# Transposing K on VectorE instead of TensorE in a one-core decode kernel, and sending one row block of a weight to half of the partitions

## The chip, the cores and the metric

The kernel runs on one core of a Trainium2 chip. The metric is device time in microseconds (us) of one execution; lower is better. The kernel before the change takes 134.09 us (median of three runs, 134.08 to 134.11). The profiled execution spans 132.1 us; all positions in time below are microseconds from the start of that span. TensorE is called PE in the profile, VectorE is DVE, ScalarE is ACT, GpSimd is POOL, and SyncE, which issues most of the transfers, is SP.

## What is computed

One decode step of a transformer layer for a batch of two tokens: attention over a sliding window of a cache, and a two-layer perceptron, both fed by the same normalised token, and added to it.

```python
# x: [2, 1, 576]; 32 query heads, 16 key/value heads of 128; the last 2048 positions of an 8192-long cache
xn = layernorm(x)
q = (xn @ wq)                                   # wq: [576, 4096]
scores = q . k_cache[:, :, 6144:, :] * 128**-0.5   # each key/value head serves two query heads
p = softmax(scores); o = p . v_cache[:, :, 6144:, :]
attn = o.reshape(2, 1, 4096) @ wo               # wo: [4096, 576]
h = relu(xn @ w1 + b1) ** 2                     # w1: [576, 4608]
mlp = h @ w2 + b2                               # w2: [4608, 576]
out = x + attn + mlp
```

All inputs are bf16. The windows of K and V are 16.8 MB each and the four weights together 20 MB, so 53.6 MB are read for very little arithmetic. (In the kernel the term x is left to the product with `sel_b`, which adds x and b2 in one matmul.)

## The kernel before

The work on the cache is cut into eight *units*: unit u holds four key/value heads of one batch element, 2 MB of K and 2 MB of V. A tile of K has 128 partitions of 64 positions times 128 elements. K must be transposed so that the head dimension lies on the partitions; the kernel before does that on TensorE, two bf16 values at a time viewed as one fp32, into PSUM, and copies the result to SBUF alternately with ScalarE and VectorE:

```python
kvpool = ctx.enter_context(tc.tile_pool(name="kvpool", bufs=6))      # six tiles for K and V together

def transposes(u, g):                            # g = 0..7
    k_f = k_tiles[u][:].bitcast(F32)
    kT_ps = psum.tile([P, JG * P], BF16, tag="kT", bufs=3, ...)
    for i in range(JG // 2):                     # four 128x128 fp32 transposes
        transpose(out=kT_f[:, i * P:(i + 1) * P], in_=k_f[:, j * P:(j + 1) * P], identity=ident_f[:])
    ...
    (nc.scalar.copy if g % 2 == 0 else nc.vector.tensor_copy)(out=kT, in_=kT_ps[:])

def scores(u, t):                                # t = 0, 1: half a unit; 8 matmuls each, four side by side
    ...
    for c in range(2):
        for g in range(4):
            matmul(sc_ps[32 * g:32 * (g + 1), :], lhsT=qz[:, tq, b, c, z:z + SR],
                   rhs=kT[:, :, 32 * g:32 * (g + 1), c], ..., tile_position=(0, 32 * g))

def softmax(u):
    # VectorE: m1 = max of the scores, m2; GpSimd: gmax = max over partitions; VectorE: gown, bias
    # ScalarE: p = exp(scale * scores + bias);  VectorE: pT = transpose(p)  (32x32 blocks)

def step(u):
    for g in range(NG):
        transposes(u, g)
        # at g = 1, 2: pv(u - 2), the product with V, and pv_end(u - 2), four VectorE operations on it
        # at g = 5: scores(u, 0);  at g = 6: fin of unit u - 2 (a matmul op_ps, then linv, om, ws on VectorE)
    scores(u, 1)
    softmax(u)
```

After unit 6 the first layer of the perceptron runs (`mlp_h`: matmuls h_ps with w1, relu on ScalarE, the square `hrow` on VectorE, its transposes `hp`, copies to `hT_sb`). Only then can the tile of w1 be given to wo. The rest of the program:

```python
mlp_h(w1_sb)
wo_sb = issue_flat(A_wo, "wo")                   # takes the buffer of w1
...                                              # w2a: first half of w2; w2b, w2c (three pieces): second half
step(NU - 1)                                     # unit 7
pv_all(NU - 2); pv_all(NU - 1)                   # V of units 6 and 7
for r in range(WR):  out_acc(ws[:, r, :], wo_sb, r)           # 128 matmuls, need `ws` of unit 7
for r in range(FR):  out_acc(hT_sb[:, 0, r, :], w2a_sb, r)    # 72 matmuls
for r in range(FR):  out_acc(hT_sb[:, 1, r, :], ...)          # 36 with w2b, 36 with w2c
nc.scalar.copy(out=fin_sb[:], in_=out_ps[:])
nc.scalar.dma_start(out=out_v, in_=fin_sb[0:RM:BS, :])
```

Each half of w2 has 18 rows (of 576 bf16, 1,152 bytes) for each of the 128 partitions. `out_acc` is four matmuls of 144 columns. Transfers are issued on SyncE's queue in this order: k0, wq, k1, v0, k2, v1, k3, v2, k4, v3, k5, v4, k6, v5, w1, k7, v6, v7, wo, w2a, w2b, w2c in three pieces.

## Time and profile before

| what | value |
|---|---|
| time, median of three runs | 134.09 us |
| span of the profiled execution | 132.1 us |
| read from HBM | 53.62 MB, 406 GB/s over the span |
| busy: PE, DVE, ACT, POOL | 84.6, 63.2, 46.7, 4.9 us |
| mean granted clock of PE | 0.834 |

The table is a summary of the page of the profile. A busy PE is not a PE at its peak, because matmuls overlap and their ends are modelled. The page's second part cuts the span into 40 slices of 3.3 us and gives the busy share of each engine in tenths; the row DMA is the mean share of the 16 transfer engines, and the row GB/s what they moved. The chain of waits follows the work that ended last backwards, from each step to what released it. A view by stretches of time gives, for any stretch, each engine's busy time with the number of instructions in brackets, then PE's granted clock, the DMA share and GB/s; its shares can pass 1 a little, since a packet counts where it starts.

### The profile page before, as it was taken

The page shows a single profiled execution, that of the slowest core. Times are in us where ns is not written, and L with a number is a line of the kernel's source. Part 1 is how long each engine was busy: PE and PEld are TensorE (multiplying, and loading weights), DVE is VectorE, ACT ScalarE, POOL GpSimd, SP SyncE. Part 2 cuts the span into 40 slices and gives each one's busy share as a digit, 9 for nine tenths or more (in the row PEclk, how much of TensorE's full clock was granted, in tenths as well). Part 3 has the DMA queues.
Part 4 walks back from the last instruction along what each step waited for, and adds up shares of the span by engine and source line. Part 5 has one row for each costly group of instructions (what it writes and reads, how often), then busy time and mean ns, then how long its engine had stood idle before and what let it go on. Part 6 is the DMA issues. An engine that isn't in the chain of part 4 may idle for free.

```text
span 132.1 us, 2285 instructions
## 1 busy us (share of the span) xinstructions
PE 84.6 (64%) x949; PEld 52.6 (40%) x949; DVE 63.2 (48%) x176; ACT 46.7 (35%) x67; POOL 4.9 (4%) x15
## 2 busy tenths in 40 slices
PE   0089319599589687697599787104819972739471
PEld 0069202286345353363455443002417640229360
DVE  7764400344557677396547687410075667550000
ACT  5725400339566085283256094200106632000000
POOL 5000000010010100100100100100000001000000
PEclk9999955959999999999779999855695999555955
DMA  4999899999999999999999999999999999899960
GB/s 160 397 437 526 369 388 442 422 432 432 429 432 422 442 417 427 437 432 437 432 427 414 437 488 402 445 424 405 427 427 442 468 435 458 376 408 418 418 255 1
DMA packets 3511, 53.76 MB, mean 407 GB/s; under 512 B 419, under 2 KB 558, under 8 KB 814
## 3 DMA queue, kind: packets, MB, share of 16 engines
q1 hardware_dynamic: 3456, 53.61, 95.2%
q8 instruction: 7, 0.11, 0.3%
q10 hardware_dynamic: 46, 0.02, 0.1%
q14 instruction: 2, 0.02, 0.0%
HBM read 53.62 MB, written 0.00 MB: 406 GB/s over the span
## 4 chain that ended last, share of the span: by engine, by line
DMA 78%; PE 15%; ACT 2%; SPq 1%; DVE 1%; issue 1%; ACTq 0%; DVEq 0%
DMA w<-in_B_w_dram 25%; DMA w2c<-in_B_w_dram 24%; DMA k<-in_A_k_cache_dram 16%; DMA wq<-in_A_wq_dram 13%; PE kT_ps L97 5%; PE h_ps L94 3%; PE q_ps L94 3%; PE sc_ps L94 2%; PE out_ps L94 1%; PE o_ps L94 1%; ACT kT L270 1%; DVE qrow L238 1%; SPq L106 0%; ACT qrow L238 0%; DVE qz L254 0%
## 5 line engine op out<-in xcount | busy, mean ns | idle before, releaser
L97 PE MATMUL kT_ps<-ident_f,k 128*128 128x128 f32 x256 | 41.4, 312 | 5.7 <-DMA k<-in_A_k_cache_dram 3.9
L97 PEld LDWEIGHTS kT_ps<-ident_f,k 128*128 128x128 f32 x256 | 32.9, 161 | 18.8 <-issue 9.9
L270 ACT COPY kT<-kT_ps 128x1024 bf16<-128x1024 bf16 x32 | 31.9, 1012 | 17.8 <-PE kT_ps L97 17.8
L272 DVE COPY kT<-kT_ps 128x1024 bf16<-128x1024 bf16 x32 | 21.8, 682 | 6.4 <-PE kT_ps L97 6.1
L94 PE MATMUL sc_ps<-kT,qz 128*32 128x512 bf16 x128 | 9.9, 388 | 6.7 <-DVE kT L272 4.7
L302 ACT ACTIVATE p<-sc_ps,bias 128x512 bf16<-128x512 f32 x8 | 5.5, 688 | 21.4 <-DVE gown L298 18.2
L94 PE MATMUL o_ps<-v,pT 128*32 128x512 bf16 x128 | 11.2, 429 | 0.0
L94 PEld LDWEIGHTS <-xnT 128*4 128x4 bf16 x108 | 3.5, 121 | 16.8 <-issue 15.2
L94 PE MATMUL h_ps<-w,xnT 128*4 128x288 bf16 x72 | 4.3, 429 | 8.0 <-DMA w<-in_B_w_dram 8.0
L305 DVE STREAM_TRANSPOSE pT<-p 128x512 bf16<-128x512 bf16 x8 | 5.7, 710 | 6.2 <-ACT p L302 6.2
L335 DVE SCALAR_TENSOR_TENSOR o<-o_ps,in_s,o 128x128 f32<-128x128 f32 x24 | 8.3, 345 | 0.4
L291 DVE TENSOR_REDUCE m<-sc_ps 128x1 f32<-128x512 f32 x8 | 5.5, 692 | 4.8 <-PE sc_ps L94 4.8
L375 DVE TENSOR_TENSOR hrow<-t 100x1152 bf16<-100x1152 f32 x2 | 2.6, 1355 | 9.6 <-ACT t L373 9.6
L94 PE MATMUL q_ps<-wq,xnT 128*4 128x512 bf16 x36 | 4.0, 627 | 4.9 <-DMA wq<-in_A_wq_dram 4.9
L295 POOL PARTITION_ALL_REDUCE gmax<-m x8 | 2.9, 367 | 104.9 <-DVE m L293 104.9
L94 PE MATMUL op_ps<-o,of_h 128*32 128x129 f32 x16 | 3.7, 316 | 4.6 <-DVE o L335 4.6
L456 ACT CAST fin_sb<-out_ps 113x144 bf16<-113x144 f32 x1 | 0.3, 280 | 17.9 <-PE out_ps L94 17.9
L94 PEld LDWEIGHTS <-qz 128*32 128x32 bf16 x128 | 2.1, 94 | 10.4 <-DVE kT L272 7.2
L97 PE MATMUL pro_ps<-ident,xn_sb 2*128 2x2 bf16 x5 | 0.9, 182 | 6.8 <-DVE xn_sb L171 6.5
L94 PEld LDWEIGHTS <-hT_sb 128*17 128x17 bf16 x144 | 3.4, 108 | 3.6 <-issue 3.5
L94 PE MATMUL out_ps<-wo,ws 128*17 128x144 bf16 x128 | 4.0, 325 | 1.2 <-DVE ws L351 1.2
L238 DVE CAST qrow<-q_ps 100x512 bf16<-100x512 f32 x1 | 0.7, 692 | 8.2 <-PE q_ps L94 8.2
(71 smaller groups left out, 57.4 us busy)
## 6 DMA issues: line engine op xcount, KB each, us to landing
k<-in_A_k_cache_dram SPq DMA_DIRECT2D x8, 2048.0 KB, 21.0
v<-in_A_v_cache_dram SPq DMA_DIRECT2D x8, 2048.0 KB, 21.5
w<-in_B_w_dram SPq DMA_DIRECT2D x1, 5184.0 KB
wq<-in_A_wq_dram SPq DMA_DIRECT2D x1, 4608.0 KB, 17.8
wo<-in_A_wo_dram SPq DMA_DIRECT2D x1, 4608.0 KB
w2a<-in_B_w_dram SPq DMA_DIRECT2D x1, 2592.0 KB, 26.9
w2b<-in_B_w_dram SPq DMA_DIRECT2D x1, 1296.0 KB
w2c<-in_B_w_dram SPq DMA_DIRECT2D x1, 864.0 KB
```

The source lines that it names most:

```text
L94: tc.keep_in_program_order(nc.tensor.matmul(*a, **k))
L97: tc.keep_in_program_order(nc.tensor.transpose(*a, **k))
L238: cp(out=qrow[:, k * QW:(k + 1) * QW].rearrange("p (i a d) -> p i a d", a=2, d=Dh), in_=q_ps[0:RB, k * QW // 2:(k + 1) * QW // 2].rearrang ...
L270: nc.scalar.copy(out=kT, in_=kT_ps[:])
L272: nc.vector.tensor_copy(out=kT, in_=kT_ps[:])
L291: nc.vector.tensor_reduce(out=m1[:], in_=sc_ps[:], axis=AX.X, op=ALU.max)
L295: nc.gpsimd.partition_all_reduce(gmax[:], m2[:], channels=P, reduce_op=ReduceOp.max)
L302: nc.scalar.activation(out=p_sb[:], in_=sc_ps[:], func=ACT.Exp, bias=bias[:, 0:1], scale=scale, accum_out=o1[:, Dh:Dh + 1])
L305: nc.vector.transpose(out=pT[:].rearrange("p j r -> p (j r)"), in_=p_sb[:])
L335: nc.vector.scalar_tensor_tensor(scalar=in_s[:, k:k + 1], in1=o1[:, 0:Dh], op0=ALU.mult, op1=ALU.add, **kw)
L375: nc.vector.tensor_tensor(out=h4[:, :, k * HB:(k + 1) * HB], in0=t4, in1=t4, op=ALU.mult)
L456: nc.scalar.copy(out=fin_sb[:], in_=out_ps[:])
```

## The change

It has two parts.

**K on VectorE.** The transposes and the copies out of PSUM go. VectorE transposes half a unit with one instruction, in blocks of 32x32, directly from SBUF to SBUF. A transpose by blocks leaves other blocks of the head dimension on each group of 32 partitions, so the query tile is laid out anew (`q_place`, one VectorE operation per unit), and a unit's scores are 16 matmuls that each fill all 128 rows and columns of the array instead of 16 that use 32 columns and run four side by side. The order on VectorE is now fixed by the program: the first half of unit u+1 is transposed ahead of the maximum of unit u, and the second half between the bias of unit u and its transposed probabilities. Unit 7 comes after the perceptron's first layer, so nothing of it is transposed ahead.

**One w2 row to half of the partitions.** Of the second half of w2, row 17 of all 128 partitions (147 KB) is no longer loaded to the partition it belongs to: it goes to partitions 0 to 63, two rows each, with four transfers of 32 partitions (`w2x`), ahead of w2b. The matching part of h is laid out the same way (`hx_sb`), and two more `out_acc` take the place of one. w2b has now 11 rows (9 before) and the three pieces of w2c 3, 2 and 1 (6, 2 and 1 before).

It is meant to relieve TensorE and ScalarE of the transposes, and to even out the load of the transfer engines at the end. Smaller things go with it: the vector b1 is loaded by eight transfers of one row (four of two rows before), and k4 is issued after unit 0.

The diff, cut to its core:

```diff
-    def transposes(u, g):
-        k_f = k_tiles[u][:].bitcast(F32)
-        kT_ps = psum.tile([P, JG * P], BF16, tag="kT", bufs=3, name=f"kT_ps_{u}_{g}")
-        ...
-        if g % 2 == 0:
-            nc.scalar.copy(out=kT, in_=kT_ps[:])
-        else:
-            nc.vector.tensor_copy(out=kT, in_=kT_ps[:])
+    def transposes(u, t):
+        kT = ktpool.tile([P, UE // NT], BF16, tag="kT_sb", name=f"kT_{u}_{t}")
+        n = UE // NT // 2
+        tc.keep_in_program_order(nc.vector.transpose(out=kT[:].bitcast(F32),
+                                                     in_=k_tiles[u][:].bitcast(F32)[:, t * n:(t + 1) * n]))
 ...
+    def q_place(u):
+        dve(nc.vector.tensor_tensor(out=qz[u % 2][...], in0=qc[:, tq, b]..., in1=own_p[:]..., op=ALU.mult))
 ...  (scores)
-        for c in range(2):
-            for g in range(4):
-                matmul(sc_ps[32 * g:32 * (g + 1), :], lhsT=qz[:, tq, b, c, z:z + SR],
-                       rhs=kT[:, :, 32 * g:32 * (g + 1), c], ..., tile_position=(0, 32 * g))
+        for i in range(NS // NT):
+            z = QO - NC * (t * NS // NT + i)
+            for h in range(2):
+                for e in range(2):
+                    matmul(sc_ps[:], lhsT=qz[u % 2][:, 2 * h + e, z:z + P], rhs=kT[:, i, :, h, :, e], ...)
 ...
+    def step(u, ahead=True):
         w = u - 2
+        if not ahead:                            # unit 7 alone
+            q_place(u)
+            for t in range(NT):
+                transposes(u, t)
+        if w >= 0:
+            pv(w)
+        for t in range(NT):
+            scores(u, t)
+        fin = pv_end(w) if w >= 0 else None
+        nxt = u + 1 < NU - 1
+        if nxt:
+            q_place(u + 1)
+            transposes(u + 1, 0)
+        rest = softmax(u)                        # m1, m2, gmax
+        if fin:
+            fin()
+        rest(transposes if nxt else None, u + 1) # gown, exp; transposes(u + 1, 1); pT
 ...
-    W2P = [(9, 15), (15, 17), (17, 18)]
-    R9 = 9
+    R9 = 11
+    RL = FR - 1
+    W2P = [(R9, 14), (14, 16), (16, RL)]
 ...
+    w2_last = w2_rows[1, :, RL * D:FR * D].rearrange("(e i q j) n -> e i j q n", e=2, i=2, q=4)
+    for i in range(2):
+        for e in range(2):
+            nc.sync.dma_start(out=w2x_sb[32 * i:32 * (i + 1), e, :], in_=w2_last[e, i])
 ...
+    for e in range(2):
+        out_acc(hx_sb[:, e, :], w2x_sb[:, e, :], 0)
-    for r in range(FR):
+    for r in range(RL):
```

## The prediction

> **What bounds the kernel now.** I read the slices first, then the transfers by stretches of time, then the chain, and last TensorE's end of the program. The slices:

> ```profile
> DMA  4999899999999999999999999999999999899960
> GB/s 160 397 437 526 369 388 442 422 432 432 429 432 422 442 417 427 437 432 437 432 427 414 437 488 402 445 424 405 427 427 442 468 435 458 376 408 418 418 255 1
> ```

> Only the first slice and the last three are not full. By stretches, the whole middle:

> ```profile
> 3.00:123.00 120.00, 80.74 (x825) 49.62 (x829) 61.18 (x163) 44.73 (x64) 2.94 (x8) 0.84 1.01 430
> ```

> For 120 us the share is 1.01 at 430 GB/s: the transfer engines never wait for a buffer, while PE is busy 67% and DVE 51%. Freeing PE and ACT in the middle therefore buys nothing by itself. What can move is the end, and there the engines do not finish together (columns: busy time of the five engines with counts, clock, DMA share, GB/s):

> ```profile
> 126.50:127.00 0.50, 0.50 (x20) 0.38 (x13) 0.00 (x0) 0.00 (x0) 0.00 (x0) 0.50 0.96 367
> 127.00:127.50 0.50, 0.08 (x4) 0.00 (x0) 0.00 (x0) 0.00 (x0) 0.00 (x0) 0.50 0.50 194
> 127.50:128.00 0.50, 0.10 (x8) 0.10 (x11) 0.00 (x0) 0.00 (x0) 0.00 (x0) 0.50 0.46 177
> 128.00:128.50 0.50, 0.50 (x24) 0.50 (x22) 0.00 (x0) 0.00 (x0) 0.00 (x0) 0.50 0.33 115
> 128.50:129.00 0.50, 0.50 (x24) 0.39 (x12) 0.00 (x0) 0.00 (x0) 0.00 (x0) 0.50 0.01 2
> ```

> The share falls to one half at 127.0 and stays near it to 128.5: half of the engines are done about 1.4 us early. Summed, 0.645 us of all engines is left after 127.0, so even a perfect balance would end near 127.7. The chain and PE's tail:

> ```profile
> 58.00 33.05 DMA w<-in_B_w_dram
> 91.09 4.30 PE h_ps L94 x71
> ...
> 96.74 31.12 DMA w2c<-in_B_w_dram
> 127.86 0.04 issue
> 127.90 1.36 PE out_ps L94 x36
> ```

> ```profile
> 118.36 4.02 PE L94 MATMUL out_ps<-wo,ws 128*17 128x144 bf16 x128 [1.16 <-DVE ws L351]
> 122.73 1.05 PE L94 MATMUL out_ps<-w2a,hT_sb 128*17 128x144 bf16 x54 [0.35 <-DMA w2a<-in_B_w_dram]
> 125.29 0.48 PE L94 MATMUL out_ps<-w2a,hT_sb 128*17 128x144 bf16 x18 [1.51 <-issue]
> 125.82 1.26 PE L94 MATMUL out_ps<-w2b,hT_sb 128*17 128x144 bf16 x36
> 127.90 1.34 PE L94 MATMUL out_ps<-w2c,hT_sb 128*17 128x144 bf16 x36 [0.82 <-DMA w2c<-in_B_w_dram]
> ```

> The last weights end the kernel, but PE waits only 0.82 us for them. Ahead of that it had no rest from the `ws` of unit 7 (ready at 118.2) on, apart from 0.35 us for w2a and a stop of 1.51 us that waits for nothing shown. So **the chain through unit 7 has less than about 1 us of slack**, and it is the one place where DVE now takes over work.

> [...] PE shows about 1,900 instructions, and the page's third part has

> ```profile
> q8 instruction: 7, 0.11, 0.3%
> ```

>  that is seven packets of 16 KB. PE's stop at 123.8 fits a block that had not come: the packet records have one at 122.85 to 123.76.
> [...]

> **The change, part by part.** The groups that go, and the row from which I take the new cost:

> ```profile
> L97 PE MATMUL kT_ps<-ident_f,k 128*128 128x128 f32 x256 | 41.4, 312 | 5.7 <-DMA k<-in_A_k_cache_dram 3.9
> L270 ACT COPY kT<-kT_ps 128x1024 bf16<-128x1024 bf16 x32 | 31.9, 1012 | 17.8 <-PE kT_ps L97 17.8
> L272 DVE COPY kT<-kT_ps 128x1024 bf16<-128x1024 bf16 x32 | 21.8, 682 | 6.4 <-PE kT_ps L97 6.1
> L305 DVE STREAM_TRANSPOSE pT<-p 128x512 bf16<-128x512 bf16 x8 | 5.7, 710 | 6.2 <-ACT p L302 6.2
> ```

> - *Removed:* 41.4 us of PE, 31.9 of ACT, 21.8 of DVE, all beside full transfers: worth 0. With 256 weight loads and 256 matmuls less, PE has about 1,400 instructions, so five instruction packets instead of seven. Each holds up one engine by some 1.4 us, [...]
> - *Added on DVE:* 16 transposes of 2,048 fp32. pT is 512 elements in 710 ns; [...] **2.3 us each**, 37 in all; `q_place` about 0.25 us each. DVE busy becomes 63.2 - 21.8 + 37 + 2 = about 80 us.
> - *DVE per unit:* two transposes 4.6, q_place 0.25, m1 and m2 0.95, four operations after V 1.5, fin 1.0, gown 0.3, pT 0.75 = **9.35 us** against 4.19 MB / 430 GB/s = **9.75 us** of transfers. It just keeps up. I place the second half of k1 at about 36 us and step on by 9.35; units 2 to 6 then lag their loads by some 9 us. Six tiles allow that: k7 needs k4's tile, free at about 63, and its turn in the queue is at about 89. Unit 6 is done near 89, ahead of w1 at 91. Worth 0.
> - *Scores:* [...] Hidden in units 0 to 6.
> - *Unit 7, exposed:* DVE comes free of `hT_sb` at 101.5; q_place to 101.8; halves at 104.1 and 106.45; scores at full clock end at 108.4 (before: 108.8). m1, m2, fin of unit 5, gown, exp, pT: to 112.3, as before (112.2). But the four operations on unit 6 now stand *behind* pT in DVE's fixed order: 112.3 to 113.85, where before they ended at 112.43. V of unit 7 waits for that PSUM tile, so `ws` comes 1.4 us later: about **119.6**. If PE's clock is at half during the scores, 1 to 1.6 us later still.
> - *w2x:* 147 KB / 430 GB/s = 0.34 us of all engines; moved from one half to the other it takes 0.34 off the slow half and adds 0.34 to the early half, which had 1.4 to spare. **-0.35 to -0.4 us** on the last landing (small packets are a little slower).
> - *PE's tail:* from ws + 0.1 there are 128 + 72 + 8 + 44 + 24 = 276 matmuls, at 31 to 35 ns some 9.1 us, with a fetch stop near the same place (about 100 matmuls before the end). With ws at 119.6: fetched block usable about 126.1, then 99 matmuls at 33 ns = 129.4, against 129.24 before; landing alone would allow 128.9.

> Sum: -0.37 us if the landing sets the end, about +0.2 with unit 7 as I place it, +1.5 with a cold clock. I take **134.2 us**.

> **Rivals.**
> 1. *The landing sets the end:* 133.7. For it: the transfers are full and the shift is sure. It needs ws by about 118.6, or a shorter fetch stop.
> 2. *PE's tail behind unit 7 sets it:* 134.1 to 136. For it: the fixed order of DVE and less than 1 us of slack. My first choice, at about 60%.
> 3. *DVE becomes the bound,* if fp32 passes at half rate (4.4 us each): 13.6 us a unit, the loads stall, over 140. Against it: a 128x32 fp32 transpose took 163 ns before the change. I give 7%.
> 4. *Less contention makes transfers faster:* against it, 430 GB/s is flat over stretches with PE busy and idle. Under 2%.

> **Range and chances.** Rival 1 gives the lower edge, 133.4 with some help of the shorter queue; a cold clock in unit 7 the upper, 136.0. Faster by over 2% needs 131.4, more than a perfect balance gives: 0.02. Slower by over 2% needs 136.8: rival 3, or both a cold clock and a longer stop: 0.10. Within 2%: 0.88.

> **What would show it.** Right: transposes of 2.2 to 2.4 us; DMA share 1.0 from 3 to 123; five q8 packets; the half-share at the end shortened to under 0.8 us; `ws` of unit 7 at 119 to 121; PE not waiting for w2c. Wrong: PE waiting for w2c (rival 1); a share below 0.95 in the middle, or transposes of 4 us (rival 3); no fetch stop in the tail.

## The result, and the profile after

The changed kernel takes **135.56 us** (median of four runs, 135.17 to 136.01) against 134.09: a ratio of 1.011, 95% interval 1.0077 to 1.0144. It is 1.5 us slower, inside the range that was predicted (133.4 to 136.0) and 1.4 us above the number itself. The profiled execution is the slowest of the four, 136.01 us with a span of 133.8; in these sessions the kernel before repeated within 0.03 us, this one varied by 0.8.

By stretches of time (columns as before: five engines with counts, clock, DMA share, GB/s), the kernel after:

```profile
3.00:123.00 120.00, 69.08 (x454) 27.20 (x458) 78.90 (x156) 14.47 (x35) 3.03 (x9) 0.83 1.01 429
127.50:128.00 0.50, 0.11 (x8) 0.00 (x0) 0.00 (x0) 0.00 (x0) 0.00 (x0) 1.00 0.54 194
128.00:128.50 0.50, 0.00 (x0) 0.00 (x0) 0.00 (x0) 0.00 (x0) 0.00 (x0) 1.00 0.33 113
128.50:129.00 0.50, 0.01 (x4) 0.01 (x3) 0.00 (x0) 0.00 (x0) 0.00 (x0) 1.00 0.22 78
129.00:129.50 0.50, 0.50 (x28) 0.38 (x31) 0.00 (x0) 0.00 (x0) 0.00 (x0) 1.00 0.05 16
```

The middle is as full as before, 1.01 at 429 GB/s, with ACT nearly empty and DVE at 78.9 us. But the last transfers end later: the share at 128.5 is 0.22, where it was 0.01, and in the packet records the last engine ends at 129.35 instead of 128.57. The chain that ended last, the kernel after:

```profile
56.34 35.79 DMA w<-in_B_w_dram
92.17 4.28 PE h_ps L96 x68
...
102.89 2.23 DVE kT L274
105.17 6.13 PE sc_ps L96 x16
...
121.78 0.38 DVE ws L359
```

Before, the chain's long step ahead of the last matmuls was the landing of w2c, which depends on nothing computed. Now it runs from w1 through the perceptron, DVE's transpose of the last K and the last scores to `ws` of unit 7: at 122.16, against 118.2. PE's end of the program (start, duration, group, what ended the idle time before it):

```profile
122.30 4.02 PE L96 MATMUL out_ps<-wo,ws 128*17 128x144 bf16 x128 [1.16 <-DVE ws L359]
126.09 1.52 PE L96 MATMUL out_ps<-w2a,hT_sb 128*17 128x144 bf16 x48
128.99 0.56 PE L96 MATMUL out_ps<-w2a,hT_sb 128*17 128x144 bf16 x24 [1.38 <-issue]
...
130.40 0.55 PE L96 MATMUL out_ps<-w2c,hT_sb 128*17 128x144 bf16 x24
```

There is no wait for w2c left, though it lands later. Only the stop of 1.38 us, in which PE waits for nothing that the profile shows, breaks the row.

**What the prediction had not seen** is why w1 lands at 92.17 and not 91.09. SP issues the loads, and its waits for transfers of b1 differ (us in all, times, longest; the kernel before, then after):

```profile
SPq L106 <- DMA b_sb<-in_B_b_dram: 6.5, 3, 2.3
```

```profile
SPq L110 <- DMA b_sb<-in_B_b_dram: 14.1, 1, 14.1
```

The issues show what the long one holds up (the issue of k1 before, then the timeline after):

```profile
2.19 0.55 SPq L106 DMA_DIRECT2D k<-in_A_k_cache_dram  x1
```

```profile
1.45 0.57 SPq L123 DMA_DIRECT2D wq<-in_A_wq_dram  x1
16.12 0.56 SPq L110 DMA_DIRECT2D k<-in_A_k_cache_dram  x1
19.08 0.54 SPq L110 DMA_DIRECT2D v<-in_A_v_cache_dram  x1
19.66 0.60 SPq L110 DMA_DIRECT2D k<-in_A_k_cache_dram  x1
```

k1 is issued at 16.12 (before: at 2.19), after 14.1 us of waiting for a transfer of b1, and the next five loads follow in a burst, from 19.08 to 21.68. Around that time the transfer engines move less, 306 GB/s instead of 386 (stretches, before and after):

```profile
18.00:20.00 2.00, 0.77 (x8) 0.24 (x11) 0.00 (x0) 0.00 (x0) 0.00 (x0) 0.50 0.90 386
```

```profile
18.00:20.00 2.00, 0.80 (x8) 0.27 (x12) 0.00 (x0) 0.00 (x0) 0.00 (x0) 1.00 0.87 306
```

The only thing that changed for b1 is that its 9 KB come in eight transfers of one row instead of four of two rows.

### The profile page after: what moved, and what is told of

The parts are those of the page before. It is cut to its first block, busy times and chain, and to the rows that moved or that the text cites. A ratio compares the mean times of both kernels' runs of the same rounds, so it can differ in the third digit from the quotient of the medians.

```text
span 133.8 us, 1760 instructions
## 1 busy us (share of the span) xinstructions
PE 75.6 (57%) x702; PEld 33.2 (25%) x702; DVE 80.9 (61%) x169; ACT 16.4 (12%) x38; POOL 5.5 (4%) x17
## 4 chain that ended last, share of the span: by engine, by line
DMA 59%; PE 17%; DVE 16%; issue 3%; SPq 2%; ACT 2%; ACTq 0%; DVEq 0%
DMA w<-in_B_w_dram 27%; DMA k<-in_A_k_cache_dram 19%; DMA wq<-in_A_wq_dram 13%; PE out_ps L96 5%; DVE kT L274 5%; PE sc_ps L96 5%; PE h_ps L96 3%; DVE o L343 2%; SPq L110 2%; PE o_ps L96 2%; DVE hrow L383 2%; DVE pT L312 1%; DVE m L294 1%; DVE hT_sb L392 1%; PE op_ps L96 1%
## 5 line engine op out<-in xcount | busy, mean ns | idle before, releaser
L96 PE MATMUL sc_ps<-kT,qz 128*128 128x512 bf16 x128 | 38.8, 458 | 16.2 <-DVE kT L274 16.1
L274 DVE STREAM_TRANSPOSE kT<-k 128x2048 f32<-128x2048 f32 x16 | 36.6, 2299 | 6.9 <-PE sc_ps L96 3.5
L96 PEld LDWEIGHTS <-qz 128*128 128x128 bf16 x128 | 13.7, 109 | 38.7 <-issue 29.3
L96 PE MATMUL o_ps<-v,pT 128*32 128x512 bf16 x128 | 12.0, 458 | 0.0
L248 DVE CAST qrow<-q_ps 100x1024 bf16<-100x1024 f32 x1 | 1.2, 1226 | 9.8 <-PE q_ps L96 9.8
L96 PEld LDWEIGHTS <-pT 128*32 128x32 bf16 x128 | 4.4, 107 | 3.7 <-issue 2.4
L96 PEld LDWEIGHTS op_ps<-o,of_h 128*32 128x32 f32 x16 | 1.3, 124 | 11.5 <-issue 10.3
L96 PEld LDWEIGHTS <-ws 128*17 128x17 bf16 x128 | 3.7, 137 | 1.6 <-issue 1.6
L96 PE MATMUL sc_ps<-ident,far_h 4*128 4x512 bf16 x8 | 3.5, 440 | 0.0
L96 PEld LDWEIGHTS <-hT_sb 128*17 128x17 bf16 x140 | 2.9, 107 | 1.6 <-issue 1.5
```

The costliest lines, as they stand in the source:

```text
L96: tc.keep_in_program_order(nc.tensor.matmul(*a, **k))
L248: cp(out=qrow[:, h * 2 * QW:(h + 1) * 2 * QW].rearrange("p (i a d) -> p i a d", a=NP4, d=HD), in_=q_v[:, h].unsqueeze(2).to_broadcast([RB, ...
L274: tc.keep_in_program_order(nc.vector.transpose(out=kT[:].bitcast(F32), in_=k_tiles[u][:].bitcast(F32)[:, t * n:(t + 1) * n]))
```

## The experiments

Each group was run beside the kernel before, which took 134.05 to 134.08 us in these sessions; the ratios are to it. "After" stands for the changed kernel.

One cost has to be known before these times are compared. The program ends with five waits of SP for completed transfers, the output's among them (waits of the queue, the kernel before, then run 9):

```profile
SPq L483 <- DMA out_dram<-fin_sb: 2.3, 1, 2.3
```

```profile
SPq L505 <- DMA out_dram<-fin_sb: 8.5, 1, 8.5
```

In the kernel before the wait for the output is the last of the five, and the other four are over while the last matmuls still run. In run 9 it is the first, and four more of 0.07 us each follow it. From the output's last packet to the end of the span it takes 1.17 to 1.18 us in the kernels before and after and in runs 3, 5 and 8, and 1.43 to 1.44 us in all the others. The first group has 32 or 40 transfers in the program, the second 36. So about 0.26 us in the time of each of the second group goes with the number of transfers and not with the part that the run is about; it is called the longer end below.

**1. b1 in four transfers again**, all else as after.

```diff
-    for i0, i1 in tuple((i, i + 1) for i in range(8)):
+    for i0, i1 in ((0, 2), (2, 4), (4, 6), (6, 8)):
```

> The changed kernel with b1 loaded by four transfers of two rows, as before, instead of eight of one row. Theory A (the end is set by unit 7's chain and TensorE's tail, and that chain starts 1.1 us late because w1 lands at 92.2 instead of 91.05; the cause of that is the late issue of k1, at 16.1 instead of 2.2, behind the eight small transfers): k1 issued at about 2, w1 lands at 91.0 to 91.2, ws of unit 7 about 1.1 us earlier, time 134.3 to 134.7. Rival B (w1 lands late for another reason, such as an instruction fetch or VectorE reading while K arrives): w1 stays at 92, time stays at 135.2 to 136.

134.99 us, ratio 1.0070 (1.0055 to 1.0085). k1 is issued at 2.27, the perceptron begins at 91.22, `ws` comes at 121.28, 0.9 us earlier. The time lies above the 134.3 to 134.7 that were expected. The rows of b1 cost 0.57 us of the 1.5, and about 0.8 once the longer end of this run is taken off; the changed kernel's own scatter (135.17 to 136.01) leaves either figure uncertain by some 0.3.

**2. The same on the kernel before**: its four transfers of b1 become eight, nothing else.

> The kernel before with b1 in eight transfers of one row, nothing else. Theory A (the late issue of k1 behind them starves some engines near 19 us and costs the transfer stream about 1 us): k1 issued at about 16, w1 lands at 92.0 to 92.3, last landing and time 0.9 to 1.2 us later, 135.0 to 135.3. Rival: only the VectorE order makes w1 late; then 134.1.

135.65 us, ratio 1.0113 (1.0095 to 1.0131): this one line is as expensive alone as the whole change, and dearer than the 0.9 to 1.2 us expected (1.3 without the longer end). k1 goes out at 16.14, the perceptron begins at 92.19, and the landing, which still bounds this kernel, is what moves (PE's end):

```profile
129.30 1.33 PE L94 MATMUL out_ps<-w2c,hT_sb 128*17 128x144 bf16 x36 [1.34 <-DMA w2c<-in_B_w_dram]
```

Before, that group began at 127.90 after a wait of 0.82. In the kernel after the same line costs less; that there the landing no longer ends last fits this. The traces show when k1 is let go. In those of the kernels before and after every landing updates one of eight counters. The counter on which k1 lands was last updated at 2.17 us in the kernel before; here it was last updated at 16.12 and in the kernel after at 16.11, by a landing of b1, and each time SP issues k1 0.01 to 0.02 us later. That the issue of k1 waits for this counter is the author's reading of these times; no run changed the number of counters itself.

**3. V of unit 6 ahead of the transposed probabilities of unit 7** in DVE's fixed order, which the prediction had blamed.

```diff
-        rest(transposes if nxt else None, u + 1)
+        rest(transposes if nxt else (None if ahead else v6), u + 1)   # v6: pv(6) and pv_end(6)
```

> The changed kernel with the four VectorE operations on V of unit 6 placed between unit 7's bias and its transposed probabilities, where VectorE waits 0.93 us for the exponential, instead of behind them. Theory A (unit 7's chain sets the end): the product with V of unit 7 starts 0.9 us earlier, time 0.6 to 0.9 us lower than the changed kernel, about 134.7. Rival C (the last transfer sets the end and the chain has slack): no difference.

135.28 us, ratio 1.0102 (1.0085 to 1.0118). `ws` comes at 119.23, 2.9 us earlier; 2.1 of these lie between the scores and `ws` (8.8 us instead of 10.9), which is what the order costs. Yet only 0.28 us are won, no more than the scatter: PE then waits for the late weights instead (0.85 us for w2a, 0.39 for w2b).

**4. Both, 1 and 3 together.**

> The changed kernel with two mends: b1 in four transfers, and the four operations on unit 6 between bias and transposed probabilities of unit 7; unit 7 still behind the perceptron's first layer. Alone they gave 134.99 and 135.28. Theory A (late landing and late chain are two separate limits, and each alone hides part of the other): together about 134.0, more than the sum of the two gains (0.57 and 0.28). If they are one and the same cause: about 134.7.

134.79 us, ratio 1.0048 (1.0032 to 1.0064). That is close to the number expected for one and the same cause, though the two gains nearly add up (0.77 together, 0.57 and 0.28 alone). `ws` at 118.48 is nearly where it was before (118.2), and 0.60 us of the span are still missing: 0.26 are the longer end, and PE's last matmul ends 0.33 later (129.58 for 129.25). PE waits 0.33 us for w2b and then has 68 matmuls left at half clock (44 with w2b took 1.50 us); the kernel before, at half clock there too, had 36 left after its last wait.

**5. Not ahead of the maximum**: the first half of the next K is transposed with the second, behind the bias.

```diff
             q_place(u + 1)
-            transposes(u + 1, 0)
 ...
             if between:
+                between(v, 0)
                 between(v, 1)
```

> The changed kernel with the first half of the next unit's K no longer transposed ahead of a unit's maximum, but together with the second half after the bias. VectorE then waits for the scores: 16 matmuls of 3.5 us at full clock, so a unit takes about 10.5 us instead of 9.4, units 2 to 6 lag 6 us more and still end ahead of w1: time within 0.5 us of the changed kernel. If TensorE, busy only some 45% of a unit, falls to half clock in the middle, scores take 6.8 us, a unit 13.7 us, and the loads stall: 145 to 160. A rival that says the order doesn't matter at all because everything is hidden expects 135.6.

135.16 us, ratio 1.0070 (1.0040 to 1.0100), with runs from 134.19 to 136.50 (the ratio leaves out the slowest). Nothing measurable is lost: that order lies beside full transfers (429 GB/s in the kernel after). The 3.5 and 6.8 us of the expectation agree with the trace of the kernel after, where half of a unit's 16 matmuls took 1.90 us at clock 1.0 (from 48.40), one starting 0.22 us after the other, and 3.57 at 0.5 (from 62.06), 0.43 apart.

**6 and 7. The w2 part taken out of after, and the w2 part alone on before.** Both were run twice, because the first pair misled. The core of the second's edit; the first is its reverse on after:

```diff
+    for i in range(2):
+        for e in range(2):
+            nc.sync.dma_start(out=w2x_sb[32 * i:32 * (i + 1), e, :], in_=w2_last[e, i])
-    for r in range(FR):
+    for e in range(2):
+        out_acc(hx_sb[:, e, :], w2x_sb[:, e, :], 0)
+    for r in range(RL):
```

> The changed kernel with row 17 of w2's second half loaded to its own partitions as before (no w2x, no hx). Theory A (TensorE's tail behind unit 7 sets the end): within 0.3 us of the changed kernel. Rival C (the landing sets the end): 0.35 to 0.4 us slower, 135.9 to 136.0 as median.

> The kernel before with the w2 part of the change alone (row 17 to partitions 0 to 63, two each; w2b 11 rows; K still transposed on TensorE, b1 in four transfers). Theory: there the landing sets the end, so 0.3 to 0.4 us faster than before, about 133.7; the stretch with half of the engines done shrinks from 1.4 us to 0.7. If TensorE's own tail has no slack left (8 more matmuls ahead of w2c), only 0.1 to 0.2. [...]

Out of after: 136.19 us, ratio 1.0153 (1.0124 to 1.0182). Alone on before: **135.58**, ratio 1.0107 (1.0087 to 1.0128), 1.5 us slower where 0.4 faster was expected, and the perceptron already began at 91.94 instead of 91.09, long before any w2 is read. The small tiles that either edit adds or removes had moved every K, V and weight tile to 32 bytes past a multiple of 64 in each partition; in the kernels before and after they lie on multiples of 512 (w2a before on one of 128). (The change cuts a spare tile at the start of SBUF from 144 floats to 112, which keeps them there.) So the next run moved the tiles alone.

**8. The kernel before, every big tile 32 bytes further.**

```diff
-    const.tile([P, 144], F32, name="pad_0")
+    const.tile([P, 152], F32, name="pad_0")
```

> The kernel before with nothing changed but the spare tile, 152 floats instead of 144: every big tile lies 32 bytes further, and no instruction differs. Theory (placement): 4.90 instead of 4.86 us per eight 16 KB packets, that is 0.8% of some 125 us of transfers, about 1.0 us: 134.9 to 135.4 us, with the first product of the perceptron at 91.8 to 92.0. Rival (placement is nothing): 134.0 to 134.2 us.

134.97 us, ratio 1.0072 (1.0058 to 1.0087), with not one instruction changed. By stretches, first the kernel before, then this one:

```profile
20.00:60.00 40.00, 32.62 (x292) 18.68 (x285) 22.70 (x58) 19.77 (x29) 1.47 (x4) 0.92 1.01 431
```

```profile
20.00:60.00 40.00, 33.48 (x285) 18.93 (x281) 21.86 (x57) 19.56 (x29) 1.46 (x4) 0.85 1.00 426
```

Both are full; the same engines move 426 GB/s instead of 431. That rate alone would not show the cause, as run 2 has 426 in this stretch too. The packets do: in the records eight of 16 KB take 4.90 us on one engine, where they take 4.86 in the kernel before and in run 2. Why the offset costs this much no run shows.

**9. Run 7 with the tiles put back**, to it:

```diff
-    const.tile([P, 144], F32, name="pad_0")
+    const.tile([P, 88], F32, name="pad_0")
```

> The kernel before with the w2 part of the change alone, as in the earlier run of it (135.58), but with the spare tile ahead of the big tiles cut from 144 to 88 floats, so that every K, V and weight tile lies at the byte offset that it has in the kernel before (a multiple of 512; in the earlier run all of them lay 32 bytes past a multiple of 64). In that earlier run eight 16 KB packets of a queue took 4.90 us instead of 4.86, and instruction packets 1.08 us instead of 0.93. Theory (placement made the surprise): 4.86 us per eight packets again, first product of the perceptron at 91.1, and 133.7 to 134.2 us. Rival (the four small w2 transfers or the order of the weights' issues make it): 135.0 to 135.6 whatever the placement.

134.40 us, ratio 1.0031 (1.0017 to 1.0046), 22 runs from 133.87 to 135.40: 1.2 us of the surprise were the placement. Of the 0.35 us above the kernel before, 0.26 are the longer end. The profiled run is the fastest of the 22. In it the shift does what it is meant to (stretches, then the chain):

```profile
128.00:128.50 0.50, 0.46 (x28) 0.28 (x16) 0.00 (x0) 0.00 (x0) 0.00 (x0) 1.00 0.28 90
128.50:129.00 0.50, 0.36 (x12) 0.09 (x3) 0.00 (x0) 0.04 (x1) 0.00 (x0) 1.00 0.00 0
```

```profile
122.05 6.58 DMA w2c<-in_B_w_dram
128.63 0.04 issue
128.67 0.27 PE out_ps L96 x4
```

By the packet records the last engine ends at 128.29 instead of 128.57, and PE's last matmul at 128.92 instead of 129.25; the longer end takes most of these 0.33 us back. What the slower runs lose no trace shows. Two steps ahead of the landing have grown in this one. PE's timeline has one that is new on the way to unit 7:

```profile
100.99 0.24 PE L99 MATMUL hx<-ident,h_last 100*64 100x100 bf16 x1 [0.74 <-ACT hT_sb L390]
101.17 1.97 PE L99 MATMUL kT_ps<-ident_f,k 128*128 128x128 f32 x8
```

The transpose for `hx_sb` makes PE wait for ACT ahead of the last K, whose transposes start at 101.17 instead of 99.94, and the matmuls with wo start 1.5 us later (119.89 against 118.36). And PE's stop in the middle of w2a, 1.51 us before, is 2.39 us here. In this run both still pass ahead of the landing; whether they make the slower runs slower was not tried.

**10. Run 6 with the tiles put back**, to it:

```diff
-    const.tile([P, 112], F32, name="pad_0")
+    const.tile([P, 168], F32, name="pad_0")
```

> The kernel after without the w2 part, as in the earlier run of it (136.19), but with the spare tile at 168 floats instead of 112, so that the K, V and weight tiles lie where the kernel after has them. Theory (placement): the 0.6 us that the earlier run lay above the kernel after were 0.8% of slower packets and are gone but for what the w2 part is really worth (0 to 0.4 us): 135.3 to 136.0 us, eight packets in 4.86 us. Rival (the w2 part is worth 0.6 us in the kernel after): 136.0 to 136.4 us.

136.19 us, ratio 1.0157 (1.0138 to 1.0175). The rival's number came, 0.6 us above the kernel after, though the two intervals overlap. Of the 0.6, 0.26 are the longer end of this run, so the w2 part saves about 0.4 us. There the late landing counts (the last packet ends at 129.99, in the kernel after at 129.35, and PE waits 0.25 us for w2c at 130.04), and DVE, not PE, leads to unit 7's scores, so the extra transpose hides. Why run 6, with its slower packets, took no longer than this one is open; its packets are slower only from about 40 us on.

**11. Unit 7 ahead of the rest of the perceptron**, with 4: DVE transposes unit 7's K before it squares h, and the copies to `hT_sb` all go to ACT.

```diff
-    mlp_h(w1_sb)                     # products, relu, square, transposes, copies
-    step(NU - 1, False)
+    mlp_h(w1_sb)                     # products, relu
+    step(NU - 1, False)              # with mlp_square() behind the transposes of K
+    mlp_transpose()                  # hp and its copies, all on ACT
+    mlp_last()                       # hx
```

(The new lines are abridged: the functions are the parts of `mlp_h`, cut where their names say.)

> The changed kernel with three mends: b1 in four transfers; the four operations on unit 6 between unit 7's bias and its transposed probabilities; and unit 7 ahead of the rest of the perceptron's first layer: after the matmuls with w1, VectorE transposes K of unit 7 at once (K lands near 96), then squares h, and the transposes and copies of h (now all copies on ScalarE) follow unit 7's exponential. Theory A: ws of unit 7 at 113 to 116, TensorE waits for every piece of w2, and the landing with the w2 shift sets the end: 133.6 to 133.8, faster than the kernel before by 0.3 to 0.5. If something else in the tail binds: 134 or more.

134.42 us, ratio 1.0020 (1.0012 to 1.0027). `ws` comes at 113.21, and PE waits for wo, w2a, w2b and, by 0.46 us, for the last of w2c. The chain through unit 7 is out of the way and the landing bounds, but the last packet ends at 128.61, not earlier than before (128.57). In the records an instruction packet of 0.90 us starts at 126.82, and a few packets of the one-row piece took more than twice their usual 51 ns; that is seen, not tested. Of the 0.35 us above the kernel before, 0.26 are the longer end.

**12. PE kept busy**: 4, plus 24 matmuls on constants between the perceptron's products and its transposes.

```diff
+        fill = psum.tile([P, NQ * B * NA * NC], F32, tag="fill", name="fill")
+        for _ in range(24):
+            matmul(fill[:], lhsT=ident[:], rhs=qc[:].rearrange("p t b a c -> p (t b a c)"), start=True, stop=True, ...)
```

> The kernel after with b1 in four transfers and the order of unit 7 changed (the earlier run of both: 134.79), plus 24 matmuls of 128x256 on constants, whose result nothing reads, on PE between the perceptron's first products and its transposes, where PE had idled for 2.9 us at a clock that had just come back to full. In the earlier run the clock fell to 0.5 when PE began again and the last scores took about 6 us. Theory (a PE that does not idle keeps its clock): the transposes and the scores of unit 7 run at 1.0, the scores take 3.5 to 4 us, and the last partial results (ws) come at 116 to 117 instead of 118.48; time 134.3 to 134.7 us, as the landing then bounds. Rival (the clock is cut however PE is kept busy): scores 6 us at 0.5, ws at 118.3 to 119.0, 134.7 to 135.0 us.

134.74 us, ratio 1.0047 (1.0034 to 1.0059), as without them. The clock stayed at 1.0 through the extra matmuls and the transposes (those took 1.33 us instead of 1.61 in the kernel after), and fell to 0.5 at about 101 all the same:

```profile
100.22 0.20 PE L101 MATMUL hx<-ident,h_last 100*64 100x100 bf16 x1 [0.92 <-ACT hT_sb L396]
103.46 5.75 PE L96 MATMUL sc_ps<-kT,qz 128*128 128x512 bf16 x16 [1.23 <-DVE kT L274]
```

Scores of 5.75 us are the rival's; `ws`, at 117.98, lies between the two. PE had waited only 0.34 and 0.92 us in the stretch of 3.41 us ahead of the fall, and was busy for 0.63 of it (last section).

No version beat the kernel before. Without the longer end runs 9 and 11 would stand at about 134.15 (an estimate), within 0.1 us of it.

## Why the prediction was right, and where not

- *Freed PE and ACT are worth 0; the middle stays full:* right, 429 GB/s against 430. Run 5 agrees.
- *Cost of a transpose:* right. 2.3 us estimated, 2,299 ns measured. No trace of the kernel before showed the estimate: it has no fp32 transpose on DVE larger than 128x32. DVE busy 80.9 us against "about 80". The rows (groups; then queues):

```profile
L274 DVE STREAM_TRANSPOSE kT<-k 128x2048 f32<-128x2048 f32 x16 | 36.6, 2299 | 6.9 <-PE sc_ps L96 3.5
```

```profile
q8 instruction: 5, 0.08, 0.2%
```

- *Five instruction packets, and the stop about 100 matmuls before the end:* right; exactly 24 + 8 + 44 + 24 matmuls follow it. In the packet records one of the five ends at 127.72, and PE goes on at 128.99; before, one ended at 123.76 and PE went on at 125.29. That PE waits there for instructions is the author's reading: the profile names nothing. The 1.4 us per packet show in the records of the kernel before: each of the first three took 0.92 to 0.96 us, and the 16 KB of data that start as it ends took 1.11 to 1.14 instead of 0.61. What two packets fewer are worth no run shows.
- *Rival 2 as first choice, PE not waiting for w2c:* right for the kernel after. The way there was in part the one named: unit 7, DVE's order, the clock. What cost most, b1, was not in it.
- *`ws` at 119.6:* wrong by 2.6 us, the step that made the number low. The scores ended at 111.29 instead of 108.4, 2.9 us late. Of these 1.08 are the landing of w1, which the working does not have at all. The other 1.8 are the clock: the number took the scores at full clock and kept 1 to 1.6 us aside for a cold one; they ran at 0.5 until 110.3 and took 6.12 us (in the kernel before 0.62 for each half, from 105.26 and 108.17). The steps from the scores to `ws` were 0.3 us shorter than worked out (10.9 for 11.2), though the order in them cost 2.1 us (run 3) and not 1.4.
- *The sum left out b1.* The eight transfers stand in the change and were passed over as a small thing. Run 1 puts 0.57 us on them in the changed kernel (about 0.8 without the longer end), run 2 1.6 in the kernel before (1.3). Without them the changed kernel takes 134.99, 0.8 above the number.
- *w2x, -0.35 to -0.4 us on the last landing:* right in sign: the last packet ends 0.28 us earlier in run 9 than in the kernel before, and 0.64 earlier in the kernel after than in run 10. In time, the longer end taken off, it costs about 0.1 us on the kernel before and saves about 0.4 on the changed one, as estimated from the medians; the scatter is nearly as large. That the row moved from the later half of the engines to the early one was the author's premise: the packet records name no engine. Small packets are slower per byte in them: 51 ns for 1,152 bytes, 93 for 2,304 and 611 for 16 KB. The extra transpose of h was not priced. The sign "half-share under 0.8 us" did not come in the kernel after: the share is between 0.54 and 0.22 from 127.5 to 129.0.
- *Rivals 3 and 4:* right to put them low; transposes of 2.3 us and not 4.4, transfers at 429 GB/s against 430.

The 1.5 us add up along three steps, with the longer end taken off where a run has it (an estimate from the medians): the rows of b1 0.83 (after to run 1, 135.56 to 134.73), the place and order of unit 7, now that DVE transposes its K, 0.57 (run 1 to run 11, 134.73 to 134.16), and all the rest, the w2 part with it, 0.09 (run 11 to the kernel before). The longer end does not show in the change itself only by chance: it brings eight transfers more, and with four more it would have had it.

## What to carry to other kernels

In this kernel, whose transfers are full from 3 to 123 us, work moved between engines was worth nothing in the middle (429 GB/s against 430). In one like it look at the two ends, at the first issues and at the chain after the last load. Read a diff's smallest line against the queue that issues the large loads: a few more transfers of 1 KB held a 2 MB load back by 14 us, and four transfers more or fewer moved the end of the program by 0.26 us. And when a variant adds a small tile, see where the large tiles end up before believing its time: here 32 bytes took 0.9 us (run 8).

## What the runs showed of the hardware

```profile
96.60:100.02 3.42, 0.48 (x11) 0.42 (x8) 2.63 (x2) 0.93 (x3) 0.00 (x0) 1.00 0.98 422
100.02:103.43 3.41, 2.68 (x32) 1.57 (x30) 2.06 (x6) 1.55 (x6) 0.00 (x0) 0.50 1.01 432
```

```profile
97.57:100.98 3.41, 2.16 (x32) 1.64 (x35) 1.69 (x6) 1.68 (x7) 0.00 (x0) 1.00 1.03 432
100.98:104.39 3.41, 2.18 (x12) 0.57 (x5) 3.41 (x3) 0.23 (x1) 0.00 (x0) 0.50 1.09 466
```

  In the stretches ahead of these two falls PE was not idle, but busy for 0.14 and 0.63 of the time.
